# Strided attention values: three residues of both heads in one product, with V block-diagonal on chip

## The chip, the cores and the metric

The kernel runs on one core of a Trainium2 chip. The metric is the device time of one execution in microseconds (us). The engines are TensorE (PE; its weight loads are listed apart as PEld), VectorE (DVE), ScalarE (ACT), GpSimd (POOL) and SyncE (SP), which issues transfers. "L450" is line 450 of the kernel before. A measurement of this kernel tells a difference of about 2% from none.

## What is computed

Attention over 8 batches, 8 heads, 576 positions and 64 dimensions, followed by a mixture of 8 experts, one for each of 4608 tokens. Four heads attend locally (the 32 positions up to the own one), four attend with stride 32: query and key must have the same residue modulo 32, so a strided head falls into 32 small causal attentions of 18 queries by 18 keys.

```python
mask_local = (rel >= 0) & (rel < stride)
mask_strided = (rel >= 0) & (pos[None, :] % stride == pos[:, None] % stride)
masks = np.stack([mask_local if h < H // 2 else mask_strided for h in range(H)], axis=0)
...
attn = attn / (np.sum(attn, axis=-1, keepdims=True) + 1e-09)
return np.matmul(attn, v).astype(np.float32)
...
    e_idx = np.argmax(logits, axis=1)
...
        h = np.maximum(x[mask] @ w1[e], 0.0)
        out[mask] = gate_w[mask, None] * (h @ w2[e])
```

## The kernel before

Work goes in units. There are 16 `Local` units (one head, two batches each) and 16 `Strided` units (two heads of one batch each), in turn. One loop over `n` issues for each step: the q and k loads of unit n + 3, the value load of unit n − 1, the scores of unit n, the transposes (`turn`) of unit n − 2 and the value products (`values`) of unit n − 3. TensorE's order is the order written in this loop (a manual schedule); a scheduler orders the other engines. `pop` puts pieces of the routing of finished batch pairs (`finish_pair`, `route`) between. When the loop is done, 18 slots of 256 tokens and one half slot go through the experts (`ffn`, `half_ffn`, lines 850 to 900), a long run of full-width matmuls.

A strided unit has 2 heads x 32 residues. `scores` leaves its exponentials in `ex`; partition 32u + a is query a of group u, and 16 columns blocks of 18 keys stand for 8 values of `i` by 2 heads; residue r is a function of `i` and `u`. `ens` holds them normalised. `turn` transposes `ens` in four pieces of 72 columns (four residue blocks of one head), so that keys lie on partitions in `ts`, and spreads each of the four 18-key blocks into a block-diagonal tile `eb` (72 partitions: 4 blocks of 18 keys), VectorE doing two of the four columns and ScalarE two (a product with a 0/1 mask, column `C_T` of the constants). `values` then has 16 matmuls: V of four residues of one head as stationary operand (`vs`, 72 keys by 64 dimensions) and one block-diagonal `eb` of 72 columns as moving operand. Head 0 writes output partitions 0 to 63, head 1 partitions 64 to 127. ScalarE copies the two outputs into `xc`, whose columns are positions, so that neighbours in the copy lie 32 floats apart. In f32, one matmul of the program is two weight loads and two matmuls in the records.

The loads of `vs` come from the SP queue into two buffers in turn; the loads of a unit wait there, in the queue's order, for the readers of the buffer two units earlier. `hh` (L789) in the half slot is a plain f32 matmul with 128 columns of weights and 128 streamed columns, `xl` and `ts` (L200, the helper `turned_to`) are f32 transposes.

Of the kernel before, what the change touches and what calls it, by code (L numbers as in the profile page):

```python
# [11 lines left out]
F32 = mybir.dt.float32  # L12
# [8 lines left out]
P = 128  # L21
# [48 lines left out]
    return (i + 2 * bb) % 18  # L70


def _constants():
    cf = np.zeros((P, C_N), np.float32)
    cf[:, C_ID:C_ID + P] = np.eye(P)
    cf[:, C_RE8:C_RE8 + E] = E - np.arange(E)
    cf[:, C_H:C_H + 2] = np.arange(P)[:, None] + P * np.arange(2)
    cf[:, C_SIO:C_SIO + 32] = np.arange(32)
    cf[:, C_P] = np.arange(P)
    cf[:, C_F:C_F + 4] = P * np.arange(4)  # L80
    for t in range(4):
        cf[18 * t:18 * t + 18, C_T + t] = 1
    cb = np.zeros((P, M_N), np.float32)
    cb[:, M_ID:M_ID + P] = np.eye(P)
    qi = np.arange(32)[:, None]
    kk = np.arange(64)[None, :]
    for m in range(4):
        for u in range(4):
            for bb in range(2):
                ok = (kk > qi) & (kk <= qi + STRIDE)  # L90
                if _block(_place(m, u), bb) == 0:
                    ok = ok & (kk >= 32)
                g = 2 * m + bb
# [12 lines left out]
    tok = P * np.arange(36)[None, :] + np.arange(P)[:, None]  # L106
    return cf, cb.astype(ml_dtypes.bfloat16), tok.astype(np.int32)


def _layout(q, k, v, moe_modality_id, moe_w_gate, moe_modality_bias, moe_w1, moe_w2):  # L110
    q, k, v = (np.asarray(t, np.float32) for t in (q, k, v))

    def local_t(t):
        return t[:, :4].reshape(NBP, 2, 4, S, D).transpose(0, 2, 1, 4, 3).reshape(NBP, 4, 2, D, 18, 32)

    qt, kt = local_t(q), local_t(k)
    vr = v[:, :4].reshape(NBP, 2, 4, 18, 32, D).transpose(0, 2, 1, 3, 4, 5)
    qkl = np.zeros((NBP, 4, 2, D, 37, 32), np.float32)  # L120
    win = np.zeros((NBP, 4, 2, 64, 20, D + 1), np.float32)
    win[..., D] = 1
    for bb in range(2):
        for i in range(18):
            blk = _block(i, bb)
            qkl[:, :, bb, :, i] = qt[:, :, bb, :, blk]
            qkl[:, :, bb, :, 19 + i] = kt[:, :, bb, :, blk]
            w = win[:, :, i % 2, :, 2 * (i // 2) + bb] if i < 16 else win[:, :, 0, :, 2 * i - 16 + bb]
            w[:, :, 32:, :D] = vr[:, :, bb, blk]
            if blk:  # L130
                qkl[:, :, bb, :, 18 + i] = kt[:, :, bb, :, blk - 1]
                w[:, :, :32, :D] = vr[:, :, bb, blk - 1]
    qkl = np.stack([qkl[:, :, 1], np.concatenate([qkl[:, :, 0, :, 18:], qkl[:, :, 0, :, :18]], axis=-2)], axis=2)
    qkl = qkl.reshape(NBP, 4, P, 37 * 32)
    vl = win.reshape(NBP, 4, P, 20 * (D + 1))

    def strided_t(t):
        t = t[:, 4:].reshape(B, 2, 2, 18, 32, D).transpose(0, 1, 2, 5, 4, 3)
        return np.ascontiguousarray(t).reshape(B, 2, 2, D, S)

    qs, ks = strided_t(q), strided_t(k)
    qks = np.stack([np.concatenate([qs[:, :, 1], ks[:, :, 1]], axis=-1), np.concatenate([ks[:, :, 0], qs[:, :, 0]], axis=-1)],
                   axis=2).reshape(B, 2, P, 2 * S)

    vs = v[:, 4:].reshape(B, 2, 2, 18, 4, 2, 4, D).transpose(0, 1, 6, 3, 4, 5, 2, 7)
    vs = np.ascontiguousarray(vs).reshape(B, 2, 72, 1024)

    w1 = np.asarray(moe_w1).reshape(E, 4, P, 8, P).transpose(0, 3, 2, 1, 4).reshape(E, 8, P, 512)
    w2 = np.asarray(moe_w2).reshape(E, 8, P, DM)
    w = np.concatenate([w1, w2], axis=-1).reshape(E, 4, 2, P, 1024).transpose(0, 1, 3, 2, 4).reshape(E * 4 * P, 2048)  # L150

    wg = np.zeros((P, 4, 32), np.float32)
    wg[:, :, :E] = np.asarray(moe_w_gate).reshape(4, P, E).transpose(1, 0, 2)
    mod = np.ascontiguousarray(moe_modality_id).astype(np.int64).view(np.int32).reshape(NT, 2)[:, 0]
    mod = mod.reshape(36, P).transpose(1, 0)
    mb = np.broadcast_to(np.asarray(moe_modality_bias).reshape(1, 2 * E), (P, 2 * E))
# [22 lines left out]
def attention_moe(ctx: ExitStack, tc: tile.TileContext, a, out):  # L179
# [79 lines left out]
    lqk = zeros(2, [P, 2, 37, 32], "lqk")  # L259
    sqk = zeros(2, [P, 96, 18], "sqk")  # L260
    ets = zeros(2, [P, 4, 4, 2, 32], "et")
    for i in range(2):
        for x in range(2):
            eng = nc.gpsimd if x else nc.vector
            pin(eng.memset(lqk[i][:, x, 0:19, :], 0.0))
            if not i and not x:

                idle = cp.tile([P, 512], BF16, name="idle")
                pin(nc.vector.memset(idle[:], 0.0))
            pin(eng.memset(sqk[i][:, 64 * x:64 * x + 32, :], 0.0))  # L270
# [2 lines left out]
        nc.tensor.matmul(warm, idle[:, 0:P], idle[:], start=True, stop=True)  # L273
    for t in ets:
        nc.vector.memset(t[:], 0.0)

    def load_qk(t, nk, src):
        w = src.shape[1]
# [102 lines left out]
    class Strided:  # L381
# [9 lines left out]

        def load_values(self):
            n = self.n
            self.vs = lp.tile([72, 8, 2, D], F32, tag="vs", name=f"vs{n}")
            ins = nc.sync.dma_start(self.vs.rearrange("p g h d -> p (g h d)"), a["vs"][self.b, self.pr])
            if n < 2:
                pin(ins)

        def scores(self):
            n, qk = self.n, self.qk  # L400
# [1 line left out]
            nc.tensor.matmul(s, identb, cb[:, M_S:M_S + 288], start=True, stop=True)  # L402
            for i in range(8):
                for u in range(4):
                    r = 16 * (i // 4) + 4 * u + i % 4
                    nc.tensor.matmul(  # L406
                        s[32 * u:32 * u + 18, 36 * i:36 * i + 36], qk[:, 32 + r, :], qk[:, r:r + 65:64, :],
                        start=False, stop=True, skip_group_check=True,
# [15 lines left out]
            nc.vector.tensor_reduce(sm[:], ex[:], AX.X, ALU.add)  # L424
            nc.vector.tensor_scalar(sm[:], sm[:], 1e-9, None, ALU.add)
            nc.vector.reciprocal(sm[:], sm[:])
            self.en = lp.tile([P, 16, 18], F32, tag="ens", name=f"ens{n}")
            nc.vector.tensor_tensor(self.en[:], ex[:], bc(sm), ALU.mult)

        def turn(self):  # L430
            n = self.n
            tp = pa(f"ts{n}").rearrange("p (g q) -> p g q", g=4)
            for g in range(4):
                turned_to(tp[0:72, g, :], self.en[:, 4 * g:4 * g + 4, :])
            self.eb = eb = lp.tile([72, 16, 4, 18], F32, tag="eb", name=f"eb{n}")
            src = tp[0:72].rearrange("p g (u x) -> p (g u) x", u=4)[:, :, 0:18]
            sh = [72, 16, 2, 18]
            nc.vector.tensor_tensor(
                eb[:, :, 0:2, :], src.unsqueeze(2).to_broadcast(sh),
                cf[0:72, C_T:C_T + 2].unsqueeze(1).unsqueeze(3).to_broadcast(sh), ALU.mult)  # L440
            for t in (2, 3):
                nc.scalar.activation(eb[:, :, t, :], src, AF.Copy, scale=cf[0:72, C_T + t:C_T + t + 1])

        def values(self):
            n, eb, vs, b = self.n, self.eb, self.vs, self.b
            for g2 in range(2):
                ot = pa(f"ot{n}{g2}")[:, :288]
                for u in range(4):
                    for h in range(2):
                        nc.tensor.matmul(  # L450
                            ot[64 * h:64 * h + 64, 72 * u:72 * u + 72],
                            vs[:, 4 * g2 + u, h, :],
                            eb[:, 4 * (2 * h + g2) + u, :, :].rearrange("p t q -> p (t q)"),
                            start=True, stop=True, skip_group_check=True,
                        )
                base = (b % 2) * S
                dst = self.xc[:, base:base + S].rearrange("p (q r) -> p r q", r=32)[:, 16 * g2:16 * g2 + 16, :]
                nc.scalar.copy(dst, ot.rearrange("p (r q) -> p r q", r=16))

    def finish_pair(bp, xt, xcs):  # L460

# [587 lines left out]
```

## Time and profile before

| | |
|---|---|
| runs shown, median (lowest to highest) | 621.11 us (620.0 to 631.92), 3 runs |
| profiled execution: time, span | 628.82 us, 627.0 us |
| TensorE busy, weight loads busy | 586.6 us (94%), 501.9 us (80%) |
| VectorE, ScalarE, GpSimd busy | 432.9 us (69%), 356.1 us (57%), 226.1 us (36%) |
| mean granted TensorE clock | 0.966 |
| first value matmul of a strided unit, last one | 21.5 us, 179.2 us |
| `vs` loads | 16 of 288 KB |

The busy times are over the whole execution. The loop over units takes about the first 182 us, the experts the rest. The busy share is a mean over both; for a change in the loop the stretch of the loop is to be read by itself. A row of the groups of instructions gives line, engine, operation, output and inputs with shapes and count, then busy time in us and the mean of one in ns, then the idle time before them and what ended it.

### The profile page before, as it was taken

To read this page: it belongs to the slowest core of one execution; us is meant where nothing else is said; L and a number is where in the kernel's file an instruction comes from. 1 tells how busy PE (TensorE), PEld (TensorE's weight loads), DVE (VectorE), ACT (ScalarE), POOL (GpSimd) and SP (SyncE) were. 2 spreads that over 40 slices of the span, in tenths; PEclk is the share of its full clock that TensorE was granted. 3 is DMA by queue.
4 is the path that set the end of the run, shared out by engine and by line. 5 is a ranking of instruction groups with operands and counts; after the bars stand their busy time and mean duration, and the time that the engine had idled before them with its cause. 6 is when DMAs were issued, how large, how long until landed. Compare 5 with 4: busy or idle time off the path is not lost.

```text
span 627.0 us, 15300 instructions
## 1 busy us (share of the span) xinstructions
PE 586.6 (94%) x6056; PEld 501.9 (80%) x6056; DVE 432.9 (69%) x1110; ACT 356.1 (57%) x739; POOL 226.1 (36%) x201
## 2 busy tenths in 40 slices
PE   7799879888889999988999999999999999999995
PEld 3577657665678888877999998989899999999985
DVE  6475645854777869948768768876877776877642
ACT  3355627444475654736556656656666665666642
POOL 1010130323163567534354345244345335513311
PEclk9898989977889999997999999999999999999999
DMA  8996787897345398394495395044045148513531
GB/s 268 296 272 199 240 283 232 272 289 280 113 170 155 114 272 248 104 210 130 112 192 194 104 260 127 6 103 103 12 92 103 40 109 226 156 27 69 184 119 54
DMA packets 66671, 102.51 MB, mean 163 GB/s; under 512 B 47327, under 2 KB 48607, under 8 KB 63008
## 3 DMA queue, kind: packets, MB, share of 16 engines
q0 software_dynamic: 19744, 58.57, 29.0%
q1 hardware_dynamic: 46560, 42.48, 28.1%
q8 instruction: 50, 0.82, 0.5%
q10 hardware_dynamic: 288, 0.41, 0.2%
q14 instruction: 29, 0.24, 0.1%
HBM read 123.66 MB, written 19.43 MB: 228 GB/s over the span
## 4 chain that ended last, share of the span: by engine, by line
PE 79%; DMA 7%; issue 5%; DVE 5%; ACT 2%; POOL 1%; SPq 0%; POOLq 0%; ACTq 0%; DVEq 0%
PE h L857 29%; PE o L871 29%; PE o L358 3%; PE s L313 3%; PE ot L450 3%; DMA cols<-rows 2%; PE ss L406 2%; PE xs L200 2%; DMA vv<-in_vl 2%; PE t L200 2%; DMA xd<-xt,posi 1%; PE ts L200 1%; PE lg L501 1%; DVE wl L893 1%; PE xl L200 1%
## 5 line engine op out<-in xcount | busy, mean ns | idle before, releaser
L893 DVE TENSOR_TENSOR wl<-raw,wh 128x512 fp32r<-128x512 f32 x288 | 187.0, 688 | 65.7 <-ACT wh L892 62.5
L892 ACT CAST wh<-raw 128x512 fp32r<-128x512 f32 x288 | 163.8, 619 | 78.5 <-PE o L871 66.6
L857 PE MATMUL h<-xh,wh 128*128 128x256 f32 x576 | 164.1, 286 | 5.9 <-ACT xh L844 3.9
L857 PE MATMUL h<-xh,wl 128*128 128x256 f32 x576 | 163.8, 285 | 0.0
L857 PE MATMUL h<-xl,wh 128*128 128x256 f32 x576 | 162.8, 283 | 0.0
L740 POOL DMA_INDIRECT raw<-in_w,wi x72 | 93.1, 1293 | 187.5 <-DVE wl L893 170.2
L857 PEld LDWEIGHTS h<-xh,wh 128*128 128x128 f32 x576 | 109.4, 190 | 13.4 <-ACT xh L844 4.6
L871 PE MATMUL o<-wh,hh 128*128 128x512 f32 x288 | 115.5, 401 | 1.1 <-ACT hh L860 1.1
L857 PEld LDWEIGHTS h<-xl,wh 128*128 128x128 f32 x576 | 109.6, 190 | 6.4
L871 PE MATMUL o<-wl,hh 128*128 128x512 f32 x288 | 114.1, 396 | 0.0
L871 PE MATMUL o<-wh,hl 128*128 128x512 f32 x288 | 111.8, 396 | 0.6 <-DVE hl L862 0.6
L857 PEld LDWEIGHTS h<-xh,wl 128*128 128x128 f32 x576 | 109.1, 190 | 1.0
L860 ACT ACTIVATE hh<-h 128x256 fp32r<-128x256 f32 x144 | 55.2, 384 | 64.6 <-PE h L857 51.7
L862 DVE SCALAR_TENSOR_TENSOR hl<-h,hh 128x256 fp32r<-128x256 f32 x144 | 60.6, 422 | 17.6 <-ACT hh L860 14.5
L577 POOL DMA_INDIRECT xd<-xt,posi x36 | 35.9, 999 | 101.3 <-DVE mxs L416 74.9
L871 PEld LDWEIGHTS o<-wh,hl 128*128 128x128 f32 x288 | 53.5, 189 | 12.0 <-DVE hl L862 0.8
L871 PEld LDWEIGHTS o<-wh,hh 128*128 128x128 f32 x288 | 54.5, 189 | 9.6 <-ACT hh L860 1.9
L871 PEld LDWEIGHTS o<-wl,hh 128*128 128x128 f32 x288 | 54.6, 190 | 5.8
L879 POOL DMA_INDIRECT out<-y,le x36 | 43.9, 1220 | 21.6 <-ACT y L878 14.9
L724 POOL DMA_INDIRECT fx<-xd,li x36 | 41.6, 1157 | 20.5 <-issue 9.8
L347 ACT COPY et<-t 64x512 f32<-64x512 f32 x32 | 18.5, 577 | 35.0 <-PE t L200 32.0
L839 DVE COPY xs<-cols 128x1024 uint16<-128x1024 uint16 x34 | 24.2, 766 | 17.3 <-DMA cols<-rows 17.3
(181 smaller groups left out, 704.0 us busy)
## 6 DMA issues: line engine op xcount, KB each, us to landing
lqk<-in_qkl SPq DMA_DIRECT2D x32, 296.0 KB
sqk<-in_qks SPq DMA_DIRECT2D x32, 288.0 KB
vv<-in_vl SPq DMA_DIRECT2D x16, 520.0 KB
vs<-in_vs SPq DMA_DIRECT2D x16, 288.0 KB
raw<-in_w,wi POOLq DMA_INDIRECT x72
vv<-in_vl SPq DMA_DIRECT2D x16, 65.0 KB
xd<-xt,posi POOLq DMA_INDIRECT x36
fx<-xd,li POOLq DMA_INDIRECT x36
```

The source lines that it names most:

```text
L200: nc.tensor.transpose(dst, src, ident)
L577: lists.add(nc.gpsimd.indirect_dma_start(xd[0:(bp + 1) * T2, :], IOA(ap=posi[:, i:i + 1], axis=0), xt[:, i, :], None))
L724: nc.gpsimd.indirect_dma_start(xt[:, h, :], None, xd[0:xrows, :], IOA(ap=li[:, s, h:h + 1], axis=0))
L740: ins = nc.gpsimd.indirect_dma_start(raws[j].rearrange("p f c -> p (f c)"), None, a["w"], IOA(ap=wi[:, s, j:j + 1], axis=0), bounds_check= ...
L839: pin(nc.vector.tensor_copy(dst, cols[:, :, w].rearrange("p h c q -> p c h q")))
L857: nc.tensor.matmul(hp, w[:, a1], x[:, c, :], start=(k == 0), stop=(k == 11))
L860: nc.scalar.activation(hh[:], hp, AF.Relu)
L862: nc.vector.scalar_tensor_tensor(hl[:], hp, 0.0, hh.bitcast(F32), ALU.max, ALU.subtract)
L871: nc.tensor.matmul(os[h], hx[:, m], w[:, 512:1024], start=(f == 0 and i == 0), stop=(f == 7 and i == 2))
L879: outs.add(nc.gpsimd.indirect_dma_start(out, IOA(ap=le[:, h, 0:1], axis=0), y[:], None, bounds_check=NT - 1, oob_is_err=False))
L892: nc.scalar.copy(wh[:, c], raw[:, c])
L893: nc.vector.tensor_tensor(wl[:, c], raw[:, c], wh[:, c].bitcast(F32), ALU.subtract)
```

## The change

Three residues instead of four go into a product, and both heads at once. Host code lays V out with the 18 keys of three residues and both heads on 108 partitions (key row times 2 plus head). On chip V is block-diagonal in the heads: of the tile `vs`, [128 partitions, 2 heads, 64 dimensions, 12 groups], the even partitions hold head 0 in the first half and the odd ones head 1 in the second, the rest stays zero from two memsets at the start. The two buffers are fixed tiles now. `ens` interleaves the heads, so one transpose takes three residues of both heads (108 columns, the last one 72): three transposes. `eb` has 108 partitions and 12 groups of 3 x 18 columns. `values` has 12 matmuls with 128 output partitions each: 8 of 108 keys by 54 columns, 4 of 72 keys by 36 columns. The weight operand of group `4g + u` is `vs[0:kn, :, :, 4g + u]`, 128 columns that lie 12 floats apart. ScalarE copies outputs of 12 and 20 residues. The loads of `vs` are two for each unit, 54 partitions of 3072 bytes, one for each head.

```diff
+def _residue(i, u):
+    return 12 * (i // 3) + 3 * u + i % 3 if i < 6 else 24 + 2 * u + i - 6
...
-    for t in range(4):
-        cf[18 * t:18 * t + 18, C_T + t] = 1
+    for t in range(3):
+        cf[36 * t:36 * t + 36, C_T + t] = 1
...
-    vs = v[:, 4:].reshape(B, 2, 2, 18, 4, 2, 4, D).transpose(0, 1, 6, 3, 4, 5, 2, 7)
-    vs = np.ascontiguousarray(vs).reshape(B, 2, 72, 1024)
+    vr = v[:, 4:].reshape(B, 2, 2, 18, 32, D)
+    vs = np.zeros((B, 2, 2, 3, 18, D, 3, 4), np.float32)
+    for i in range(8):
+        for u in range(4):
+            vs[:, :, :, i % 3, :, :, i // 3, u] = vr[:, :, :, :, _residue(i, u)]
+    vs = vs.reshape(B, 2, 2, 54, 768)
...
+    vss = zeros(2, [P, 2, D, 12], "vs")
...
+    for t in vss:
+        nc.gpsimd.memset(t[:], 0.0)
...
-            self.vs = lp.tile([72, 8, 2, D], F32, tag="vs", name=f"vs{n}")
-            ins = nc.sync.dma_start(self.vs.rearrange("p g h d -> p (g h d)"), a["vs"][self.b, self.pr])
+            self.vs = vss[n % 2]
+            for h in range(2):
+                ins = nc.sync.dma_start(
+                    self.vs[h:108:2, h].rearrange("p d g -> p (d g)"), a["vs"][self.b, self.pr, h])
...
-            self.en = lp.tile([P, 16, 18], F32, tag="ens", name=f"ens{n}")
-            nc.vector.tensor_tensor(self.en[:], ex[:], bc(sm), ALU.mult)
+            self.en = lp.tile([P, 8, 18, 2], F32, tag="ens", name=f"ens{n}")
+            nc.vector.tensor_tensor(self.en.rearrange("p i k h -> p h i k"),
+                                    ex.rearrange("p (h i) k -> p h i k", h=2),
+                                    sm.rearrange("p (h i) -> p h i", h=2).unsqueeze(3).to_broadcast([P, 2, 8, 18]),
+                                    ALU.mult)
...
-            for g in range(4):
-                turned_to(tp[0:72, g, :], self.en[:, 4 * g:4 * g + 4, :])
-            self.eb = eb = lp.tile([72, 16, 4, 18], F32, tag="eb", name=f"eb{n}")
+            for g in range(3):
+                en = self.en[:, 3 * g:min(3 * g + 3, 8)].rearrange("p i k h -> p (i k h)")
+                turned_to(tp[0:en.shape[1], g, :], en)
+            self.eb = eb = lp.tile([108, 12, 3, 18], F32, tag="eb", name=f"eb{n}")
...
-            for t in (2, 3):
-                nc.scalar.activation(eb[:, :, t, :], src, AF.Copy, scale=cf[0:72, C_T + t:C_T + t + 1])
+            nc.scalar.activation(eb[:, 0:8, 2, :], src[0:108, 0:8, :], AF.Copy, scale=cf[0:108, C_T + 2:C_T + 3])
+            sh = [72, 4, 2, 18]
+            nc.vector.tensor_tensor(
+                eb[0:72, 8:12, 0:2, :], src[0:72, 8:12].unsqueeze(2).to_broadcast(sh),
                 cf[0:72, C_T:C_T + 2].unsqueeze(1).unsqueeze(3).to_broadcast(sh), ALU.mult)
...
-            for g2 in range(2):
-                ot = pa(f"ot{n}{g2}")[:, :288]
-                for u in range(4):
-                    for h in range(2):
+            for gs, r0, rn in (((0,), 0, 12), ((1, 2), 12, 20)):
+                ot = pa(f"ot{n}{r0}")[:, :18 * rn]
+                q0 = 0
+                for g in gs:
+                    w, kn = (54, 108) if g < 2 else (36, 72)
+                    for u in range(4):
                         nc.tensor.matmul(
-                            ot[64 * h:64 * h + 64, 72 * u:72 * u + 72],
-                            vs[:, 4 * g2 + u, h, :],
-                            eb[:, 4 * (2 * h + g2) + u, :, :].rearrange("p t q -> p (t q)"),
+                            ot[:, q0:q0 + w], vs[0:kn, :, :, 4 * g + u].rearrange("p h d -> p (h d)"),
+                            eb[0:kn, 4 * g + u, :, :].rearrange("p t q -> p (t q)")[:, 0:w],
                             start=True, stop=True, skip_group_check=True,
                         )
```

TensorE, in the second strided unit's step of the loop, before: the transposes of the scores of a local unit (`t`), the value products of the first strided unit (`ot`), the mask and scores of a later unit (`ss`), the transposes of a strided unit (`ts`). A row gives line, operation, output and inputs, output shape and count.

```order
L200 MATMUL t_407<-cf_sb,ex_235 128x128 x4
L200 MATMUL t_412<-cf_sb,ex_235 64x128
L450 MATMUL ot_418<-eb_335,vs_233 64x72 x8
L450 MATMUL ot_428<-eb_335,vs_233 64x72 x8
L402 LDWEIGHTS cb_sb
L402 MATMUL ss_443<-cb_sb 128x288
L406 MATMUL ss_443<-sqk_86 18x36 x32
L200 MATMUL ts_488<-cf_sb,ens_328 72x128 x4
```

The same place in the changed kernel:

```order
L209 MATMUL t_410<-cf_sb,ex_239 128x128 x4
L209 MATMUL t_415<-cf_sb,ex_239 64x128
L474 MATMUL ot_421<-eb_338,vs_90 128x54 x4
L474 MATMUL ot_427<-eb_338,vs_90 128x54 x4
L474 MATMUL ot_427<-eb_338,vs_90 128x36 x4
L416 LDWEIGHTS cb_sb
L416 MATMUL ss_442<-cb_sb 128x288
L420 MATMUL ss_442<-sqk_86 18x36 x32
L209 MATMUL ts_487<-cf_sb,ens_332 108x128 x2
L209 MATMUL ts_487<-cf_sb,ens_332 72x128
```

The order of TensorE's groups is the same; 16 value matmuls of half the output partitions are 12 of all of them, and four transposes are three.

SP's queue at the second strided unit's value load, before (`lqk`, `sqk` are queries and keys, `vv` the local values):

```order
L279 DMA sqk_87<-in_qks 64x1152
L280 DMA sqk_87<-in_qks 64x1152
L395 DMA vs_371<-in_vs 72x1024
L296 DMA vv_440<-in_vl 128x1040
L299 DMA vv_440<-in_vl 64x260
```

And in the changed kernel:

```order
L291 DMA sqk_87<-in_qks 64x1152
L292 DMA sqk_87<-in_qks 64x1152
L408 DMA vs_91<-in_vs 54x768 x2
L291 DMA lqk_84<-in_qkl 64x1184
L292 DMA lqk_84<-in_qkl 64x1184
L308 DMA vv_439<-in_vl 128x1040
L311 DMA vv_439<-in_vl 64x260
```

One load of 72 rows is two of 54 rows, and here the local values come behind the next local queries and keys instead of ahead of them; later in the loop the order of the other loads is as before.

More of the change, by code (lines that the diff above doesn't have):

```diff
@@ L393, in load_values @@
             n = self.n
-            self.vs = lp.tile([72, 8, 2, D], F32, tag="vs", name=f"vs{n}")
-            ins = nc.sync.dma_start(self.vs.rearrange("p g h d -> p (g h d)"), a["vs"][self.b, self.pr])
-            if n < 2:
-                pin(ins)
+            self.vs = vss[n % 2]
+            for h in range(2):
+                ins = nc.sync.dma_start(
+                    self.vs[h:108:2, h].rearrange("p d g -> p (d g)"), a["vs"][self.b, self.pr, h])
+                if n < 2:
+                    pin(ins)
         def scores(self):
@@ L404, in scores @@
                 for u in range(4):
-                    r = 16 * (i // 4) + 4 * u + i % 4
+                    r = _residue(i, u)
                     nc.tensor.matmul(
@@ L430, in turn @@
         def turn(self):
             n = self.n
-            tp = pa(f"ts{n}").rearrange("p (g q) -> p g q", g=4)
-            for g in range(4):
-                turned_to(tp[0:72, g, :], self.en[:, 4 * g:4 * g + 4, :])
-            self.eb = eb = lp.tile([72, 16, 4, 18], F32, tag="eb", name=f"eb{n}")
[L436 to L439, printed above, removed]
+            tp = pa(f"ts{n}")[:, 0:384].rearrange("p (g q) -> p g q", g=3)
@@ new lines, in turn @@
+            for g in range(3):
+                en = self.en[:, 3 * g:min(3 * g + 3, 8)].rearrange("p i k h -> p (i k h)")
+                turned_to(tp[0:en.shape[1], g, :], en)
+            self.eb = eb = lp.tile([108, 12, 3, 18], F32, tag="eb", name=f"eb{n}")
+            src = tp.rearrange("p g (u x) -> p (g u) x", u=4)[:, :, 0:18]
+            sh = [108, 8, 2, 18]
+            nc.vector.tensor_tensor(
+                eb[:, 0:8, 0:2, :], src[0:108, 0:8].unsqueeze(2).to_broadcast(sh),
+                cf[0:108, C_T:C_T + 2].unsqueeze(1).unsqueeze(3).to_broadcast(sh), ALU.mult)
@@ L444, in values @@
         def values(self):
             n, eb, vs, b = self.n, self.eb, self.vs, self.b
-            for g2 in range(2):
-                ot = pa(f"ot{n}{g2}")[:, :288]
-                for u in range(4):
-                    for h in range(2):
+            base = (b % 2) * S
+            for gs, r0, rn in (((0,), 0, 12), ((1, 2), 12, 20)):
[4 more added lines that the diff above has]
+                    for u in range(4):
@@ L455, in values @@
                         )
-                base = (b % 2) * S
-                dst = self.xc[:, base:base + S].rearrange("p (q r) -> p r q", r=32)[:, 16 * g2:16 * g2 + 16, :]
-                nc.scalar.copy(dst, ot.rearrange("p (r q) -> p r q", r=16))
+                        q0 += w
+                dst = self.xc[:, base:base + S].rearrange("p (q r) -> p r q", r=32)[:, r0:r0 + rn, :]
+                nc.scalar.copy(dst, ot.rearrange("p (r q) -> p r q", r=rn))
     def finish_pair(bp, xt, xcs):
```

## The prediction, made before the changed kernel ran

> **What bounds the kernel now.** I read the busy shares first, then a table by stretch of time, then the chain of waits inside the attention stretch, then the waits of TensorE alone. The sum is made against the profiled execution: span 627.0 us, its own time 628.82 us, 7.7 us above the median of 621.11 us of the runs shown (620.0 to 631.92). I take differences from the trace and add them to the median.
>
> ```profile
> span 627.0 us, 15300 instructions
> PE 586.6 (94%) x6056; PEld 501.9 (80%) x6056; DVE 432.9 (69%) x1110; ACT 356.1 (57%) x739; POOL 226.1 (36%) x201
> core 0: us, PE busy (x) PEld busy (x) DVE busy (x) ACT busy (x) POOL busy (x), PEclk, DMA share, GB/s
> 13.00:60.00 47.00, 39.08 (x922) 29.04 (x922) 27.53 (x94) 22.70 (x54) 2.11 (x3) 0.89 0.90 268
> 60.00:120.00 60.00, 53.44 (x1250) 40.38 (x1248) 36.98 (x147) 34.67 (x82) 11.09 (x13) 0.97 0.77 244
> 120.00:182.00 62.00, 53.39 (x973) 40.40 (x974) 36.26 (x167) 29.95 (x69) 20.35 (x22) 0.83 0.65 221
> 182.00:627.00 445.00, 430.84 (x2753) 386.83 (x2751) 323.27 (x683) 265.58 (x532) 189.91 (x154) 0.99 0.50 131
> ```
>
> Columns of the last four rows: the stretch, its length, then busy time and count for each engine, TensorE's granted clock, the DMA share and rate. The edit lives in attention, 13 to 182 us; the 445 us behind it are expert matmuls that it does not touch and that start in TensorE's program order when attention ends. So the question is what 169 us of attention become. TensorE is busy there for 39.08 + 53.44 + 53.39 = 145.9 us (86%); VectorE 60%, ScalarE 52%.
>
> ```profile
> by line: PE o L358 12.2%; issue 11.1%; PE s L313 10.8%; PE ot L450 9.6%; PE ss L406 7.1%; DMA vv<-in_vl 6.3%; PE t L200 5.7%; PE xs L200 5.3%; PE ts L200 4.6%; PE xl L200 4.3%; PE lg L501 3.3%; PE s L309 3.1%; PE o L369 2.4%; PE s L320 1.5%
> PE s L313 <- issue: 8.0, 9, 3.9
> PE ss L406 <- issue: 4.3, 8, 1.2
> PE ot L450 <- issue: 2.3, 5, 0.7
> PE s L320 <- issue: 1.5, 4, 0.5
> PE t L200 <- issue: 1.3, 2, 0.8
> ```
>
> The first row is the chain in that stretch: TensorE's lines fill most of it, no ScalarE or VectorE line is among the largest, and one DMA (`vv`) is. The other rows are TensorE's idle time: 17.4 us in which it "waited for nothing that the profile shows", inside runs of like matmuls, while the DMA share was high. So time added to TensorE here passes to the end, except what it takes out of these 17.4 us.
>
> **The value matmuls (`ot`), the term that decides.** They are on the chain with 9.6%.
>
> ```profile
> 13.00:182.00 169.00, 21.97 (x512) 18.89 (x512) 0.90 0.76 242
> L450 PEld LDWEIGHTS ot<-eb,vs x512: 132/137/230, 21.5 to 179.1; 72*64 72x64 f32 x171
> L789 PEld LDWEIGHTS hh<-xhh,raw x64: 187/192/192, 604.6 to 618.0; 128*128 128x128 f32 x64
> 34.47 1.15 PE ot L450 x32
> 604.88 1.05 PE L789 MATMUL hh<-xhh,raw 128*128 128x128 f32 x8
> L789 PE MATMUL hh<-xhh,raw x64: 270/275/275, 604.9 to 618.1; 128*128 128x128 f32 x64
> ```
>
> Row one is line 450 alone: 21.97 us of TensorE in 512 records, so 32 records and 1.37 us for each of 16 units; the code has 16 matmuls a unit, so an f32 matmul is two weight loads and two matmul records. Rows two and three give minimum, median and maximum of a weight load: 137 ns at 64 columns, 192 at 128, so 64 more columns cost 55 ns, 0.86 ns a column. A 64-column load therefore takes 55 ns and 32 in turn would take 1.76 us, but the undisturbed piece in row four did all 32 in 1.15 us. So the two heads, which write different halves of the output partitions, load and run **beside each other**.
>
> The change gives that up. It has 12 matmuls, 24 records, each with 128 weight columns over the whole width: 128 x 0.86 = 110 ns to load. `hh` (plain f32, full width, another 128x128) confirms the pace from outside: (1.05 − 0.275) / 7 = 111 ns from one matmul to the next. That pace could also be its 128 streamed rows, so 0.87 ns a row at most; 54 rows stream in 47 ns and hide under the next load. The load is the limit: 24 x 0.111 = **2.66 us a unit where 1.37 stood, +1.29, times 16 = +20.6 us**, even if each load is no dearer than `hh`'s.
>
> **The step of 12 in V.** The new weights are `vs[0:kn, :, :, 4g + u]`: 128 columns that lie 12 floats (48 bytes) apart, where both rows above read neighbours. No weight load of before has such a step. Lower bound: no charge, 111 ns. The upper bound comes from an engine that does step:
>
> ```profile
> L458 ACT COPY xc<-ot 128x288 f32<-128x288 f32 x32 | 20.1, 662 | 2.1 <-remote 2.1
> L474 ACT COPY xc<-xl 128x512 f32<-128x512 f32 x12 | 6.9, 598 | 0.5 <-PE xl L200 0.4
> L474 ACT COPY xc<-xl 128x128 f32<-128x128 f32 x6 | 1.6, 272 | 0.0
> ```
>
> Both lines copy PSUM into `xc`; line 474 writes neighbours, line 458 writes every 32nd float. Line 474: (598 − 272) / 384 = 0.85 ns an element and 163 ns fixed. Line 458: (662 − 163) / 288 = 1.73 ns, **twice as much**. Doubled loads take 220 ns: 24 x 0.22 = 5.28 us a unit, +3.91, times 16 = +62.6 us. A write by ScalarE is not a read by TensorE, but it is the only f32 row here with such a step, so I take the doubled value and keep the plain one as lower end.
>
> The Trainium skill, "SBUF — State Buffer", section "Specifications (TRN2)", speaks against this layout: lines there are 16 bytes, an access pattern needs at least two hits in a line for full bandwidth, and each step to a new line pays. V's step of 48 bytes hits each line once. ScalarE's 0.85 against 1.73 ns agrees with that rule; whether weight loads follow it no row of before shows. By the rule the sum is the dear one, +62.6; without it +20.6.
>
> **The other edits.**
>
> ```profile
> 43.29 0.63 PE L200 MATMUL ts<-cf_sb,ens 128*72 128x128 f32 x4
> L200 PE MATMUL ts<-cf_sb,ens 128*72 128x128 f32 x64 | 11.2, 303 | 1.0 <-DVE ens L428 1.0
> L438 DVE TENSOR_TENSOR eb<-ts,cf_sb 72x576 f32<-72x576 f32 x16 | 12.0, 751 | 2.6 <-PE ts L200 2.1
> L419 DVE TENSOR_TENSOR exs<-ss,mxs 128x288 f32<-128x288 f32 x16 | 7.2, 450 | 0.2
> L442 ACT ACTIVATE eb<-ts,cf_sb 72x288 f32<-72x288 f32 x32 | 14.2, 493 | 10.9 <-DVE eb L438 10.1 <-DVE xt L548 0.5 <-ACT exs L422 0.2
> L265 POOL MEMSET lqk<- 128x608 f32 x2 | 1.2, 608 | 0.3 <-POOLq L1041 0.3
> 13.01 0.60 SPq L395 DMA_DIRECT2D vs<-in_vs  x1
> vs<-in_vs SPq DMA_DIRECT2D x16, 288.0 KB
> SPq L395 <- PE ot L450: 19.2, 9, 13.5
> ```
>
> *Transposes.* Four take 0.63 us, so (0.63 − 0.303) / 3 = 0.11 us each; one less in 16 units is −1.75 us.
>
> *VectorE.* From 450 ns at 288 elements and 751 at 576: 1.05 ns an element, 149 ns fixed. The two new `eb` products (288 and 144 elements) take 450 + 300 = 750 ns, as the one did. `ens` keeps 288 elements and writes every second float: 0 to +0.25 us a unit (the doubled slope), up to 4 us on an engine 60% busy; I take 0.
>
> *ScalarE.* Two copies of 493 ns become one with half the elements, near 300 (`L474` at 128: 272): −0.69 us a unit. The `xc` copies of 216 and 360 elements cost 537 + 786 = 1323 ns against 2 x 662. ScalarE is not on the chain, so 11 us of relief count 0. `values` runs a step after `turn`, which covers `eb` on both engines.
>
> *GpSimd.* Two memsets of 1536 columns, about 1.5 us each by line 265's 1 ns a column, end near 6 us; the first `vs` transfer is issued at 13.01. Covered by 7 us; uncovered it would cost 3 once.
>
> *Transfers.* 2 x 54 x 3072 bytes = 324 KB where 288 stood: 0.59 MB more in all, 2.4 us at 242 GB/s. SP issues one more (0.33 to 0.60 us each). `vs` waits on SP until the value matmuls two units earlier have read its buffer (last row), and the next q, k and `vv` loads queue behind it; slower matmuls hold that up by as much as they hold up the readers. I take 0 of 0 to +2.4: with TensorE 20 to 60 us longer, transfers have more room.
>
> **Sum.** +62.6 − 1.75 = +60.9 us on TensorE. Of the 17.4 us of idle issue I let half, 9, go under the longer matmuls: **+52 us**, 628.82 to about 681 for a profiled run like this one and 621.11 to **673**.
>
> **Rivals.** *Plain loads:* the step costs nothing. +20.6 − 1.75 = +18.9, less 3 of the idle issue (a third of the 9, as the added time is a third): +16, **637 us** (631 to 643). For it: both weight-load rows are unit step and TensorE's reading port isn't ScalarE's writing port. *Not slower:* full-width loads might go faster than `hh`'s. The transposes' loads do:
>
> ```profile
> L200 PEld LDWEIGHTS xl<-cf_sb,xt 128*128 128x128 f32 x72 | 7.7, 141 | 0.6
> ```
>
> 141 ns for 128 columns against 192 at `hh`, so 110 − 51 = 59 ns a load, 24 x 0.059 = 1.42 us a unit: a draw, and with the transposes −1 us, **620**. It decides below 57 ns a load (1.37 / 24); at best the stream rules, 16 x 0.047 + 8 x 0.031 = 1.0 us, −5.9 − 1.75 = −7.7, 613, short of 2%. Against it: `hh`'s loads are the plain f32 form that `ot` uses, and all 64 lie within 187 to 192. *Transfers become the bound:* `vs` arrives late for the chain's 6.3% of `vv`; +2.4 on top of either case.
>
> **How the numbers follow.** Doubled loads 0.52 (655 to 690: idle issue given back from nothing to all 17, `ens` and transfers added), plain loads 0.34, not slower 0.10, dearer than doubled 0.04. Forecast 673; the range 631 to 690 takes in the first two and leaves out about 0.18. The 2% that a measurement can tell from no change are 12.4 us: plain loads fall within it at their lower edge (0.04), so within 2% is 0.12, faster 0.02 (the 613 with luck in the idle issue), slower 0.86.
>
> **What would show it.** `ot` weight loads median near 300 ns (192 + 110) if doubled, 192 if plain, about 140 if not slower; the value matmuls' busy TensorE time near 84, 43 or 22 us in all. Attention ends near 182 + 52 = 234 us, and the 445 us behind it stay. ScalarE's `eb` loses about 10 us without effect. If attention lengthens but `ot` doesn't, the transfers did it. If `ot` lengthens and the end does not, TensorE wasn't the bound and I misread the chain.

## The result and the profile after

The changed kernel takes **694.96 us** (median of 4 runs, 693.06 to 701.75) against 623.93 us (4 runs, 620.0 to 631.92): ratio **1.1166**, 95% interval 1.1104 to 1.1228, 71 us slower. Some executions of a kernel are slow, over 1.5% above its fastest one; medians here and below are of all runs, ratios of the fast ones. The profiled execution took 693.1 us with a span of 691.2, 64.2 us more than the span of before: the traced run of before lies 4.9 us above its median of 623.93, that of the changed kernel 1.9 below its own, so the traces account for 64 of the 71 us.

The page of the changed kernel: span, busy time of each engine, TensorE's busy share and its granted clock in 40 slices, and the two groups of line 474, which is line 450 of before.

```profile
span 691.2 us, 15019 instructions
PE 676.4 (98%) x5912; PEld 598.6 (87%) x5912; DVE 429.5 (62%) x1126; ACT 354.6 (51%) x723; POOL 230.8 (33%) x203
PE   6999999999999999999999999999999999999996
PEclk9687886787887679999999999999999999999999
L474 PE MATMUL ot<-eb,vs 108*128 108x54 f32 (+1 forms) x384 | 104.9, 439 | 0.8 <-issue 0.7
L474 PEld LDWEIGHTS ot<-eb,vs 108*128 108x128 f32 (+1 forms) x384 | 104.3, 369 | 1.3 <-issue 1.2
```

TensorE was busy 94% and is now busy 98%. Value matmuls fill 104.9 us where 21.97 stood, and the weight loads of the same line are busy for all but 0.6 us of that: the loads set the pace. In the clock's row, nearly all slices of attention (the first 14 or so) stand at 6 to 8 tenths, those of the experts at 9.

The table by stretch, of the changed kernel and then of before, each cut where its own attention ends (length, busy time and count of each engine, granted clock, DMA share, rate):

```profile
13.00:253.10 240.10, 237.06 (x2989) 207.19 (x2990) 98.55 (x426) 85.30 (x188) 36.94 (x40) 0.76 0.56 180
253.10:691.20 438.10, 429.61 (x2760) 386.18 (x2758) 322.02 (x682) 266.04 (x531) 188.60 (x151) 0.99 0.49 128
```

```profile
13.00:181.10 168.10, 145.00 (x3135) 108.91 (x3134) 99.87 (x405) 86.41 (x202) 32.90 (x37) 0.90 0.76 242
181.10:627.00 445.90, 431.74 (x2758) 387.74 (x2758) 324.17 (x686) 266.48 (x533) 190.55 (x155) 0.99 0.50 131
```

Attention grew from 168.1 to 240.1 us. Inside it TensorE's busy time went from 145.0 to 237.06 and its idle time from 23.1 to 3.0; VectorE, ScalarE and GpSimd kept theirs to within 4 us. The granted clock fell from 0.90 to 0.76. The experts' stretch is 7.8 us *shorter*.

| term, us of span | predicted | measured |
|---|---|---|
| value matmuls, 21.97 → 104.89 | +62.6 | +82.9 |
| TensorE's other work in attention, 123.0 → 132.2 | −1.75 | +9.1 |
| TensorE idle in attention, 23.1 → 3.0 | −9 | −20.1 |
| experts, 445.9 → 438.1 | 0 | −7.8 |
| sum | +52 | +64.2 |

The chain of waits in 13 to 250 us and one of its pieces (start, length), then all that TensorE waited for there (us, times, longest):

```profile
by line: PE ot L474 43.0%; PE o L370 11.9%; PE s L325 7.8%; PE ss L420 6.5%; PE xl L209 4.7%; PE t L209 4.5%; PE ts L209 4.2%; PE xs L209 3.7%; PE s L321 2.8%; DMA vv<-in_vl 2.7%; PE lg L524 2.4%; PE o L381 2.2%; PE ss L416 1.4%; PE lt L209
36.28 6.38 PE ot L474 x24
```

```profile
PE ts L209 <- DVE ens L442: 1.0, 1, 1.0
PE ot L474 <- issue: 0.7, 2, 0.5
PE o L370 <- DMA vv<-in_vl: 0.6, 1, 0.6
PE ss L420 <- issue: 0.5, 1, 0.5
```

`ot` went from 9.6% to 43.0% of the chain. The 24 records of a unit take 6.38 us, 0.266 each, where the forecast had 0.220. "Issue", 17.4 us before, is 1.2 us here and no longer among the chain's large entries.

The longest idle time of TensorE in the experts' stretch, before and after (the last number of a row is the idle time, with what ended it), and what it goes back to before:

```profile
L857 PE MATMUL h<-xh,wh 128*128 128x256 f32 x576 | 164.1, 286 | 5.9 <-ACT xh L844 3.9
L839 DVE COPY xs<-cols 128x1024 uint16<-128x1024 uint16 x34 | 24.2, 766 | 17.3 <-DMA cols<-rows 17.3
L880 PE MATMUL h<-xh,wh 128*128 128x256 f32 x576 | 163.4, 284 | 0.4 <-ACT xh L867 0.4
```

Before, TensorE waits once for 3.9 us for `xh`, the tokens of a slot, which VectorE and ScalarE make from the transfer `cols<-rows`; after, 0.4 us. That is 3.5 of the 5.7 us by which TensorE's idle time behind attention shrank (14.2 to 8.5).

The products and copies beside the matmuls (count, then minimum, median and maximum of one in ns):

```profile
L474 PEld LDWEIGHTS ot<-eb,vs x384: 341/369/373, 22.9 to 250.0; 108*128 108x128 f32 x128, 72*128 72x128 f32 x64
L456 DVE TENSOR_TENSOR eb<-ts,cf_sb x16: 448/458/460, 15.9 to 239.9; 108x288 f32<-108x288 f32 x16
L459 ACT ACTIVATE eb<-ts,cf_sb x16: 364/381/382, 16.4 to 240.4; 108x144 f32<-108x144 f32 x16
L461 DVE TENSOR_TENSOR eb<-ts,cf_sb x16: 264/295/299, 18.2 to 241.4; 72x144 f32<-72x144 f32 x16
L442 DVE TENSOR_TENSOR ens<-exs,sms x16: 447/450/524, 14.8 to 234.7; 128x288 f32<-128x288 f32 x16
```

A weight load of `ot` shows 369 ns where `hh` shows 192: 177 more, not the 110 of a doubled load. The other rows came near their forecast: `eb` on VectorE takes 458 + 295 = 753 ns (750), `ens` 450 as before, `eb` on ScalarE 381 (300).

### The profile page after: what moved, and what is told of

Its sections match the earlier page's. It is cut to its first block, busy times and chain, and to the rows that moved or that the text cites. A ratio compares the mean times of both kernels' runs of the same rounds, so it can differ in the third digit from the quotient of the medians.

```text
span 691.2 us, 15019 instructions
## 1 busy us (share of the span) xinstructions
PE 676.4 (98%) x5912; PEld 598.6 (87%) x5912; DVE 429.5 (62%) x1126; ACT 354.6 (51%) x723; POOL 230.8 (33%) x203
## 4 chain that ended last, share of the span: by engine, by line
PE 84%; DVE 6%; DMA 5%; issue 3%; ACT 0%; POOL 0%; SPq 0%; POOLq 0%; DVEq 0%; ACTq 0%
PE h L880 25%; PE o L894 24%; PE ot L474 15%; PE o L370 4%; DMA cols<-rows 3%; PE s L325 3%; DVE wl L916 3%; PE ss L420 2%; PE xl L209 2%; PE xs L209 2%; PE t L209 2%; PE ts L209 1%; PE lg L524 1%; PE s L321 1%; DMA vv<-in_vl 1%
## 5 line engine op out<-in xcount | busy, mean ns | idle before, releaser
L474 PE MATMUL ot<-eb,vs 108*128 108x54 f32 (+1 forms) x384 | 104.9, 439 | 0.8 <-issue 0.7
L474 PEld LDWEIGHTS ot<-eb,vs 108*128 108x128 f32 (+1 forms) x384 | 104.3, 369 | 1.3 <-issue 1.2
L430 DVE TENSOR_REDUCE mxs<-ss 128x16 f32<-128x288 f32 x16 | 7.3, 458 | 81.7 <-PE ss L420 81.7
L902 POOL DMA_INDIRECT out<-y,le x36 | 45.0, 1250 | 21.6 <-ACT y L901 14.2
```

The source lines that it names most:

```text
L474: nc.tensor.matmul(ot[:, q0:q0 + w], vs[0:kn, :, :, 4 * g + u].rearrange("p h d -> p (h d)"), eb[0:kn, 4 * g + u, :, :].rearrange("p t q - ...
L902: outs.add(nc.gpsimd.indirect_dma_start(out, IOA(ap=le[:, h, 0:1], axis=0), y[:], None, bounds_check=NT - 1, oob_is_err=False))
```

## The experiments

The runs were made on three chips (sets 3 and 4 on the same one), on which the median of the kernel before was 606 to 629 us, so times are compared inside a set, by their ratio to the kernel before. Three questions: what part of the load's price is the step, what part the full width; what else the longer loads do to TensorE; and why 71 us came out of 83.

### Set 1: the step alone, and the added time alone (before: 610.74 us)

**Step 1.** V lies group by group, so that the 128 weight columns are neighbours; its zeros come with the transfer, which doubles it to 648 KB a unit.

```diff
-    vss = zeros(2, [P, 2, D, 12], "vs")
+    vss = zeros(2, [P, 12, 2, D], "vs")
...
+            ins = nc.sync.dma_start(self.vs[0:108].rearrange("p g h d -> p (g h d)"), a["vs"][self.b, self.pr])
...
-                            ot[:, q0:q0 + w], vs[0:kn, :, :, 4 * g + u].rearrange("p h d -> p (h d)"),
+                            ot[:, q0:q0 + w], vs[0:kn, 4 * g + u].rearrange("p h d -> p (h d)"),
```

> The changed kernel with the same 12 full-width matmuls, but V laid out so that the 128 weight columns of a matmul are neighbours (step 1 instead of 12). V comes with its zeros in one load of 648 KB a unit instead of two of 162 KB, and the memsets write the same tiles. Theory A (the step of 12 makes the loads dear, full width makes the rest): matmuls of ot 111 ns apart instead of 267, ot busy near 43 us instead of 104.9, time near 637 us, 13 to 20 above the kernel before. Theory B (the full-width f32 load is itself dear when little streams under it): still near 267 ns apart, time near 695. Theory C (full width costs nothing): time at or under the kernel before.

**Steps 2 and 4.** The twelve groups are cut in sets of s = 2 or 4 that lie side by side, so that weight columns are s floats apart; transfers have the size of the changed kernel's.

```diff
-    vss = zeros(2, [P, 2, D, 12], "vs")
+    vss = zeros(2, [P, 12 // s, 2, D, s], "vs")
...
-                            ot[:, q0:q0 + w], vs[0:kn, :, :, 4 * g + u].rearrange("p h d -> p (h d)"),
+                            ot[:, q0:q0 + w], vs[0:kn, (4 * g + u) // s, :, :, (4 * g + u) % s].rearrange("p h d -> p (h d)"),
```

> The changed kernel with weight columns 2 floats (8 bytes) apart; V's loads write runs of 512 bytes. Theory A1 (a charge for each new 16-byte line, two hits in a line are enough): loads 111 ns apart, ot busy near 43 us. Theory A2 (any step other than 1 is charged): 267 ns apart, ot busy near 105 us. Theory A3 (the charge grows with the lines touched): between, near 140 ns.

> The changed kernel with weight columns 4 floats (16 bytes) apart; V's loads write runs of 1 KB. Theory A1 and A2: as with 12, 267 ns apart, ot busy near 105 us. A charge that grows with the distance beyond one line: clearly less, 150 to 220 ns. No charge up to 4 floats: 111 ns.

The value matmuls' weight loads at step 1, step 2 and step 4:

```profile
L475 PEld LDWEIGHTS ot<-eb,vs x384: 186/192/338, 20.9 to 176.8; 108*128 108x128 f32 x128, 72*128 72x128 f32 x64
```

```profile
L474 PEld LDWEIGHTS ot<-eb,vs x384: 194/196/198, 21.5 to 169.2; 108*128 108x128 f32 x128, 72*128 72x128 f32 x64
```

```profile
L474 PEld LDWEIGHTS ot<-eb,vs x384: 307/329/332, 19.9 to 231.8; 108*128 108x128 f32 x128, 72*128 72x128 f32 x64
```

At step 1 the load is `hh`'s to the nanosecond (192), step 2 costs 4 ns more, step 4 137 more. Busy time of the value matmuls: 48.75, 46.91 and 91.44 us; the first two stand against a forecast of 43, as the records come 122 to 127 ns apart and not 111. **The step is what makes the load dear**, and it isn't the mere fact of a step. The times were 637.79 us at step 1 (632.77 to 641.5; ratio 1.0565, 1.0448 to 1.0682), 611.82 at step 2 and 674.38 at step 4 (one run each). The 637 us expected for step 1 were met in the absolute only, on a chip where the kernel before is faster: the ratio stands for some 34 us more, not 13 to 20.

Step 1 is slower than step 2, with the same load and the same work on TensorE. Its own is the transfer of twice the size: the DMA share in its attention is 0.87.

```profile
13.00:178.50 165.50, 154.48 (x2970) 129.84 (x2957) 97.14 (x422) 81.42 (x186) 34.96 (x38) 0.93 0.87 284
178.50:630.90 452.40, 432.25 (x2760) 387.04 (x2758) 322.44 (x684) 267.32 (x533) 192.74 (x153) 0.99 0.50 128
```

Against step 2's span of 609.8 us (attention to 171.3) that is 7 us more in attention and 14 more in the experts' stretch, where TensorE is idle for 20 us. So 324 KB more a unit go with 21 us in the traces and 26 in the times; that the transfers cause it was not tested apart. The part behind attention can't be their direct competition, as the last of them was issued at 165.5 us; TensorE's wait for `xh` is 9.6 us there, 1.0 at step 2.

**The old product twice.** The kernel before with each of its value matmuls issued two times, to see what added TensorE time is worth.

```diff
-                for u in range(4):
+                for u in list(range(4)) * 2:
```

> The kernel before with each strided value matmul written twice (the second writes the same result again): 16 matmuls more a unit, 1.0 us by the undisturbed pace of 62 ns for a pair of records, 16 to 18 us in all. It prices TensorE time added in attention. Theory P (TensorE is the bound, little hides): +13 to +18 us. Theory H (the added time first fills TensorE's idle issue of 17 us): +0 to +6 us.

```profile
13.00:172.20 159.20, 146.65 (x3620) 118.19 (x3607) 99.04 (x405) 88.80 (x202) 34.25 (x38) 0.96 0.77 257
```

The value matmuls went to 39.15 us, some 18 more, and the time to 622.2 us (618.56 to 629.26; ratio 1.0326, 1.0186 to 1.0465), 11 us more at the lower end of the interval and 28 at the upper: added TensorE time in attention does pass to the end here, 11 of 18 us at the least.

### Set 2: the halves, the stream and a closer look at step 2 (before: 606.31 us, 19 runs)

**Step 2 again, in five rounds**, as in set 1, and **before once more**, for a trace on the same chip.

> The kernel with weight columns 2 floats apart again, timed against the kernel before. Its one look gave loads 118 ns apart: 24 x 118 = 2.83 us a unit where 1.37 stood, +23.4 us of TensorE less 1.75 for the transposes. Theory P (added TensorE time passes to the end but for the idle issue): +4 to +19 us. Theory H (what it adds is hidden as long as idle issue and transfers leave room): within 2% of the kernel before.

> The kernel before once more, for a trace from the same chip as its neighbours: attention ends near 170 to 181 us, value matmuls 22 us busy, idle issue of TensorE 10 to 25 us.

The table by stretch, of step 2 and then of before, both cut at 609 us:

```profile
13.00:172.30 159.30, 152.19 (x2990) 127.89 (x2989) 96.84 (x424) 81.87 (x186) 34.89 (x38) 0.96 0.82 262
172.30:609.00 436.70, 428.32 (x2760) 385.31 (x2758) 323.51 (x684) 267.67 (x533) 188.89 (x153) 1.00 0.50 132
```

```profile
13.00:161.80 148.80, 132.73 (x3084) 102.29 (x3079) 98.96 (x404) 86.48 (x201) 32.68 (x36) 0.93 0.84 271
161.80:609.00 447.20, 430.74 (x2760) 386.43 (x2758) 322.93 (x685) 266.74 (x533) 193.83 (x155) 0.99 0.52 131
```

611.87 us (609.5 to 635.7, 10 runs), ratio 1.0076, 1.0029 to 1.0123: below one per cent, some 5 us. The value matmuls take 47.38 us against 20.84, +26.5. By the times, then, about a fifth of the added time reached the end here, where it was most of it in the old product twice. What decides between the two was not found.

Where the rest went, these two traces can't settle. That of before is of a run of 613.3 us, 1.9% above the fastest of its set, with the lower clock in attention (0.93 against 0.96), and is even the longer one (spans of 611.4 and 609.6 us). As they stand, step 2 has 7.1 us less of TensorE's other work (fewer transposes, the higher clock), 9.0 less of idle time in attention (16.1 to 7.1), and 10.5 less in the experts' stretch, with 8.4 us of TensorE idle in it instead of 16.5. TensorE's wait for `xh` is 8.7 us of that in before, and step 2 has none.

**Halves.** Step 1 without the full width: each head's 64 columns into its own half of the output, 24 matmuls.

```diff
-    vss = zeros(2, [P, 2, D, 12], "vs")
+    vss = zeros(2, [P, 2, 12, D, 1], "vs")
...
+                        for h in range(2):
+                            nc.tensor.matmul(
+                                ot[64 * h:64 * h + 64, q0:q0 + w], vs[0:kn, h, 4 * g + u, :, 0],
...
```

> The changed kernel with 24 value matmuls of 64 columns, each head into its own half of the output partitions as before, on all 108 keys (the other head's rows of V are zero), and columns that are neighbours. Theory of the halves (loads of the two halves run beside each other): pairs of records about 57 ns apart, 48 records in 1.4 us a unit, ot busy 22 to 26 us, time within 1% of the kernel before. If the full key depth of 108 rows or the zeros matter: near the 43 us of full width.

```profile
L475 PEld LDWEIGHTS ot<-eb,vs x768: 132/138/227, 20.7 to 166.3; 108*64 108x64 f32 x129, 72*64 72x64 f32 x63
```

```profile
13.00:167.00 154.00, 135.58 (x3364) 106.36 (x3358) 96.52 (x418) 77.71 (x184) 32.55 (x36) 0.94 0.81 267
```

Twice as many records, of 138 ns, take 26.14 us, 1.63 us a unit, where the full-width loads of step 2 take 2.96. **Two 64-column loads in different halves do run beside each other**, as the prediction had read from 32 records in 1.15 us, and full width gives that up. The time is 613.77 us (610.35 to 624.02, 10 runs), ratio 1.0141, 1.0096 to 1.0186, no better than step 2 although its value matmuls are 21 us shorter. Its TensorE is idle for 18.4 of the 154 us, step 2's for 7.1 of 159.3: so far down, shorter value matmuls mostly turn into idle time.

**A longer stream.** In the changed kernel, seven of the twelve matmuls of a unit stream two groups (108 columns) instead of one; what the second group writes is overwritten by the next matmul.

```diff
-                            ot[:, q0:q0 + w], vs[0:kn, :, :, 4 * g + u].rearrange("p h d -> p (h d)"),
+                            full[:, q0:q0 + (108 if 4 * g + u < 7 else w)],
+                            vs[0:kn, :, :, 4 * g + u].rearrange("p h d -> p (h d)"),
+                            eb[0:kn, 4 * g + u:4 * g + u + 2, :, :].rearrange("p g t q -> p (g t q)") if 4 * g + u < 7
...
```

> The changed kernel (step 12) with 7 of its 12 value matmuls streaming 108 columns instead of 54 under the same loads; the extra columns are overwritten by the next matmul. Streaming 108 columns takes 95 ns, well under a load. Theory K (TensorE's clock falls in attention because the array stands still under long loads, and that costs time): granted clock in attention above the 0.72 to 0.81 of the changed kernel and 3 to 10 us faster. Theory L (the clock is not what costs): no change in time, loads 267 ns apart.

```profile
L475 PEld LDWEIGHTS ot<-eb,vs x384: 341/369/373, 22.3 to 246.3; 108*128 108x128 f32 x128, 72*128 72x128 f32 x64
```

The loads are the changed kernel's (369), the value matmuls' busy time too (104.49 us): the stream hides under the load. The time is 689.8 us (688.59 to 691.95), ratio 1.1385, 1.1283 to 1.1486, and the clock in attention 0.80. The changed kernel did not run on this chip, so the two can't be compared here; if the clock follows the share of time in which the array streams, this stream was too short to show it.

### Set 3: the clock, and more steps (before: 629.32 us)

**Every value matmul streams its columns four times**, 216 and 144 columns instead of 54 and 36, under the same load; the copies are overwritten or not read.

```diff
-                            ot[:, q0:q0 + w], vs[0:kn, :, :, 4 * g + u].rearrange("p h d -> p (h d)"),
-                            eb[0:kn, 4 * g + u, :, :].rearrange("p t q -> p (t q)")[:, 0:w],
+                            full[:, q0:q0 + 4 * w], vs[0:kn, :, :, 4 * g + u].rearrange("p h d -> p (h d)"),
+                            eb[0:kn, 4 * g + u, :, :].rearrange("p t q -> p (t q)")[:, 0:w].unsqueeze(1).to_broadcast([kn, 4, w]),
```

> The changed kernel (step 12) in which each value matmul streams its columns four times over (216 or 144 columns, 180 or 120 ns at full clock, where 54 or 36 stood), all still under a load of 267 ns; the repeats are overwritten by the next matmul. Theory K (TensorE's clock falls because its array stands still under long loads): granted clock in attention back to 0.9 or more, the other TensorE work of attention 10 to 18 us shorter, loads perhaps at the 233 ns of step 4, time near 675 us by a kernel before of 624, or 8 to 25 us under the changed kernel. Theory L (the clock follows the loads and not the streaming): clock stays at 0.72 to 0.82, time unchanged.

```profile
L475 PEld LDWEIGHTS ot<-eb,vs x384: 341/369/373, 21.4 to 227.8; 108*128 108x128 f32 x128, 72*128 72x128 f32 x64
```

672.22 us (670.32 to 673.49), ratio 1.0752, 1.0645 to 1.0859, with loads of the same 369 ns and a clock of 0.98 in attention. Four times the arithmetic, and *less* time than any run of the changed kernel took (689.05 us and up). The comparison on one chip is in set 4.

**Steps 6 and 3**, with the diff of set 1 and s = 6 and 3.

> The changed kernel with weight columns 6 floats (24 bytes) apart. Steps 4 and 12 gave 233 and 267 ns. If the charge beyond one line grows with distance: 235 to 250 ns. If it is one more step at some distance or alignment: 233 or 267.

> The changed kernel with weight columns 3 floats (12 bytes) apart: three of four loads of a float touch a new 16-byte line. A charge for each new line, by steps 2 (one new line in two, 118 ns) and 4 (one in one, 233 ns): 0.75 x 233 = 175 ns. A threshold on the step below 16 bytes: 118 ns.

```profile
L474 PEld LDWEIGHTS ot<-eb,vs x384: 296/317/319, 21.2 to 233.1; 108*128 108x128 f32 x128, 72*128 72x128 f32 x64
```

```profile
L474 PEld LDWEIGHTS ot<-eb,vs x384: 250/262/337, 20.8 to 207.9; 108*128 108x128 f32 x128, 72*128 72x128 f32 x64
```

Step 6 shows 317 ns (677.06 us, one run), step 3 262 ns (649.72 us, one run): three floats lie between the free and the dear ones. From record to record step 3 takes 183 ns (table in set 4), near the 175 expected of a charge for each new line; step 6, at 227, lies a little under all that was expected.

**The old product with step 8.** The kernel before, V laid out so that its 64 weight columns are 8 floats apart.

```diff
-            self.vs = lp.tile([72, 8, 2, D], F32, tag="vs", name=f"vs{n}")
+            self.vs = lp.tile([72, 2, D, 8], F32, tag="vs", name=f"vs{n}")
...
-                            vs[:, 4 * g2 + u, h, :],
+                            vs[:, h, :, 4 * g2 + u],
```

> The kernel before with V's weight columns 8 floats (32 bytes) apart, all else as it was. If the charge falls on each load and the two halves still load beside each other: pairs of records 115 to 135 ns apart instead of 62, ot busy 32 to 36 us instead of 22, weight loads at 190 to 205 ns. If the halves no longer overlap: 230 ns and more for a pair, ot busy 60 us or more.

```profile
L450 PEld LDWEIGHTS ot<-eb,vs x512: 194/218/223, 21.4 to 183.6; 72*64 72x64 f32 x171
```

218 ns where 137 stood, 81 more for 64 columns; the value matmuls' busy time is 35.67 us for 512 records, 70 ns each: the halves still overlap, and the step charges there as well. One run: 634.99 us.

### Set 4: the clock on one chip, and a step of 16 (before: 629.01 us)

**The changed kernel again**, **the fourfold stream again** (diff in set 3), and V's rows padded from 12 to **16 floats**:

```diff
-    vss = zeros(2, [P, 2, D, 12], "vs")
+    vss = zeros(2, [P, 2, D, 16], "vs")
```

> The changed kernel again, for a comparison on one chip with the four-fold stream: 1.10 to 1.125 of the kernel before, granted clock 0.76 in attention.

> The four-fold stream again beside the changed kernel. Theory K: 20 to 28 us under the changed kernel on the same chip, clock near 0.98 in attention, loads still 267 ns apart. Theory L (the difference between 1.117 and 1.075 came from the chips): the two within 1.5% of each other.

> The changed kernel with V's rows padded from 12 to 16 floats (64 bytes between weight columns; loads of 4096 bytes a row). Distance theory (the charge goes on growing beyond one line): over 267 ns between loads, 290 or more. Alignment theory (steps of 16 and 32 bytes took 1.82 ns a column, 48 bytes 2.09, as an odd number of lines): 225 to 235 ns. A plateau from 48 bytes on: 267.

The attention stretch of the changed kernel, all work and line 474 alone, then the same two of the fourfold stream (line 474 alone: length, then PE, PEld and ScalarE time, clock, DMA share, rate):

```profile
13.00:248.00 235.00, 231.64 (x2925) 201.69 (x2926) 96.70 (x416) 82.37 (x184) 37.33 (x40) 0.78 0.55 181
13.00:248.00 235.00, 105.00 (x384) 104.31 (x384) 21.03 (x32) 0.78 0.55 181
```

```profile
13.00:232.00 219.00, 209.96 (x2972) 184.44 (x2957) 101.78 (x430) 86.78 (x192) 37.51 (x41) 1.00 0.60 199
13.00:232.00 219.00, 105.96 (x384) 104.19 (x384) 21.60 (x32) 1.00 0.60 199
```

The changed kernel took 693.11 us (689.05 to 698.35; ratio 1.1064, 1.0986 to 1.1141), the fourfold stream 673.56 us (670.55 to 675.25; ratio 1.0708, 1.0655 to 1.0762): **19.5 us less for an edit that only adds streamed columns**. The value matmuls cost the same (105.00 and 105.96 us), so these loads don't follow the granted clock. All else on TensorE shrinks from 231.64 − 105.00 = 126.6 to 104.0 us while the clock goes from 0.78 to 1.00; 5.7 us of that come back as idle time. In the changed kernel a 54-column stream keeps the array at work for about 47 of each 270 ns (estimate from 0.87 ns a row of `hh`), and the clock that is granted falls for all TensorE work around it. The Trainium skill, "TensorE: Matmul & The Clock Gate", section "Part 1: The HAM clock gate (the "warmup" mystery)", lets the clock depend on how busy TensorE has been of late; these two runs agree, and in them the time under a weight load with nothing streaming did not keep the clock up.

```profile
L474 PEld LDWEIGHTS ot<-eb,vs x384: 291/311/331, 22.7 to 232.8; 108*128 108x128 f32 x128, 72*128 72x128 f32 x64
```

Step 16 (676.31 us, one run) is *cheaper* than step 12: 311 against 369 ns. All full-width f32 loads of 128 columns together:

| step in floats | load, median ns | value matmuls, us busy | by 384 records, ns | clock in attention |
|---|---|---|---|---|
| 1 | 192 | 48.75 | 127 | 0.93 |
| 2 | 196 | 46.91 | 122 | 0.96 (set 2) |
| 3 | 262 | 70.09 | 183 | 0.86 |
| 4 | 329 | 91.44 | 238 | 0.78 |
| 6 | 317 | 87.10 | 227 | 0.78 |
| 12 | 369 | 104.89 | 273 | 0.76 |
| 16 | 311 | 85.44 | 223 | 0.78 |

## Why the prediction was right and wrong

**Right: the direction and its mechanism.** TensorE bounds attention, so its added time reached the end; the chain and the waits of after say so (its idle time there is 3.0 of 240.1 us). The halves did overlap and full width gives that up (halves, set 2). The step charges the load (sets 1, 3, 4). The rivals with plain and with cheap loads fall to the 369 ns, and so does the rival in which transfers become the bound: the DMA share fell from 0.76 to 0.56, and TensorE's longest wait for a transfer is 0.6 us.

**Wrong: the step of 12, taken at 220 ns.** The term came out at +82.9 us, not +62.6. Some 4 to 6 of the 20 us missing are the plain price, 47 to 49 us of value matmuls at steps 2 and 1 where 43 stood; the other 14 to 16 are the charge for the step, 56 to 58 us where the forecast had 42. A doubled load was nearly the right size for steps 4, 6 and 16 (85.4 to 91.4 us of value matmuls, forecast 84). At step 2 there is no charge, and of that ScalarE's row, with its step of 32 floats, could say nothing. The Trainium skill's rule of "SBUF — State Buffer", section "Specifications (TRN2)", fits this: 16-byte lines and two hits in each give steps 1 and 2 full speed; at step 3 four columns share three lines, and it lies between; from 4 on each column has a line of its own. But 12 floats cost 13 to 20 us above that in all, and neither the step's length (16 is cheaper) nor the count of lines explains it. The thought that an odd number of lines in a step pays extra gave the right 225 to 235 ns for step 16 (223), but step 4 is an odd number too, one line, and does not pay it (238). **The cause of this last fifth stays open.** What sets 48 bytes apart from 16, 24 and 64 was not tried further.

**Wrong: no term for the clock.** The sum priced TensorE's other work in attention at −1.75 us, and it came out at +9.1. The granted clock went from 0.90 to 0.76, and set 4 shows the mechanism, where TensorE's other work takes 126.6 us at 0.78 and 104.0 at 1.00: against a full clock it costs 19.5 us. In the forecast the 54-row stream "hides under the next load", which is right for its own time; that an array hidden under loads is granted less clock was missed.

**Wrong in size: the idle time.** Half of the 17.4 us of issue was let go, 9 us. Nearly all went, 16.2, and 20.1 of TensorE's idle time in all; why was not tested. A lower DMA share isn't needed for it: step 2 has only 7.1 us of idle time at a share of 0.82. And the 445 us behind attention did not stay: 7.8 us less, with 8.5 us of TensorE idle time in them instead of 14.2, most of it by the shorter wait for `xh`. The loads and the clock made the sum 31 us too small; these two terms, together 19 us too large, cancelled more than half of it. That the traced difference, +64 us, came so near to +52 is in that part luck.

**Wrong: the level.** The forecast added a difference of traces to the median of 621.11 us, but the traced run of before stood 7.7 us above that median, and the trace of after stands 1.9 under its own. These 10 us are the rest of the 22 between 673 and 694.96. With the measured +64 in place of +52 the same step gives 685, inside the range; its upper end of 690 had room for all of the idle time, but none for loads beyond 220 ns or for the clock.

**Small things.** `ens`, `eb` on VectorE, the memsets and SP's queue cost nothing, as forecast. ScalarE's `eb` takes 381 ns instead of 300 and saved about 8 us instead of 10, without effect. Attention ended near 253 us, not 234, by the terms above.

**Open:** how much of added TensorE time reaches the end. It was most of it with the old product twice, a fifth with step 2, 64 of 92 us (82.9 + 9.1) with the change. The experts' stretch was 8 to 10 us shorter with both of the latter, and TensorE's wait for `xh`, that is for the transfer `cols<-rows`, is the largest piece of it. That wait is 3.9 to 8.7 us in the four traces with the old product, 9.6 at step 1, 4.8 in one of the two with the fourfold stream, and 1.3 or less in all the others; why the transfer is late in some was not tested.

No version tried beats the kernel before: step 2 is nearest with a ratio of 1.0076.

## What to carry to other kernels

Price a weight load by how its columns lie, not by their count alone: here a load of 128 f32 columns took 192 to 196 ns at a step of 1 or 2 floats and 311 to 369 from 4 on, and laying V out in pairs of groups took the cost of the change from 11.7% to 0.8%. Before one full-width product replaces two half-width ones, look whether the two run beside each other; 32 records in 1.15 us told it. And when a change lengthens loads on the engine that bounds, read the granted clock of that stretch as a term of its own: the work around the loads pays too.

## What the hardware showed that was not expected

- Streaming four times as many columns under the same loads made the kernel 19.5 us faster: clock 1.00 instead of 0.78 in attention, other TensorE work 104.0 instead of 126.6 us (set 4). Doubling the stream in seven of twelve matmuls left the clock at 0.80.
- Weight loads at a step of 12 did not follow that clock: 105.00 us at 0.78, 105.96 at 1.00.
- A step of 12 floats costs more than 16: 369 against 311 ns a load, 104.89 against 85.44 us.
